# Zeroing two key buffers later on GpSimd, with a new written-out order of all operations, in a two-layer attention and token-MLP kernel

## The chip, the core and the metric

The kernel runs on one core of a Trainium2 chip. The metric is device microseconds of one execution. Four runs of the kernel before gave 458.5, 462.82, 458.71 and 455.29 us, a median of 458.61 us. The core has a matrix engine (TensorE, "PE" in the profile), three engines for elementwise work (VectorE "DVE", ScalarE "ACT", GpSimd "POOL") and a sync engine (SyncE, "SP", whose queue of DMA issues is "SPq").

## The reference

The input `x` has 2048 tokens of 512 numbers, in bf16. Two equal layers follow one another. The first half of a layer is causal attention in a sliding window of 256 tokens, with 32 heads of 16 numbers; the second is an MLP that mixes tokens.

```python
def _A_ref(x, wqkv, wo):                       # attention, H = 32, Dh = 16, W = 256
    qkv = (x @ wqkv).reshape(B, S, 3, H, Dh)   # then q, k, v per head
    scores = einsum("bhqd,bhkd->bhqk", q, k) * Dh ** -0.5
    mask = (i - j >= 0) & (i - j < W)
    p = softmax(where(mask, scores, -1e9))
    return einsum("bhqk,bhkd->bhqd", p, v) ... @ wo

def _B_ref(x, w1, b1, w2, b2):                 # token-mixing MLP, F = 1792
    u = gelu(einsum("bsd,sf->bdf", layernorm(x), w1) + b1)
    return transpose(einsum("bdf,fs->bds", u, w2) + b2)

for _ in range(2):
    x = x + _A_ref(layernorm(x), A_wqkv, A_wo)
    x = x + _B_ref(layernorm(x), B_w1, B_b1, B_w2, B_b2)
```

## The kernel before

**Tiles.** The 2048 tokens lie in `x_sb` as 16 blocks of 128 tokens on the partitions. Four blocks make a group `m`. A block is normalised on VectorE: statistics (`stat`, L479), their aggregate (`agg`, L481), the power -1/2 on GpSimd (`rstd`, L492) and a subtract-and-multiply into `xh_sb` (`xh`, L499). The first group is turned by TensorE (`ftr`, L557) and copied to `xhT` (`evt`, L564 and L566); later groups are turned by DMA (`tr`, L550). Projections give q, k and v (`fq`, `fk` through L521, `fv` L627).

**The key buffers.** Keys go into `kbd`, three slots of 128 x 4096 bf16 in a block-diagonal form: for each head pair, the half that belongs to the other head must be zero. The first group writes its slot in full from PSUM, times a 0/1 column (`evka`, L587 and L589). Later groups put the keys into a staging tile `stg` (`evk`) and then into `kbd` (`kz`), in one of three ways: eight small DMAs that write only the own half (L607), or two multiplications by the 0/1 column on GpSimd or VectorE (both L612). The DMAs need the rest of the slot to be zero, so slots 1 and 2 are zeroed once (`zk`, L461), and every `kz` waits for that. The ones columns in the value buffers `vb` are written once too (`one`, L465 on GpSimd or VectorE, L468 on ScalarE).

**Attention.** A layer has 76 score steps (`sc`, L690). Each fills four PSUM banks, and ScalarE turns them into probabilities with two exponentials (`exp`, L705); GpSimd multiplies the diagonal parts by a mask (`mask`, L723); TensorE multiplies by the values (`pv`, L740). VectorE transposes the sums (`od`, L760), takes reciprocals (`rec`, L764), GpSimd or VectorE multiplies (`prod`, L766), VectorE transposes back (`od2`, L771). The output projection (`fwo`) is added to `x_sb` (`res`, L782).

**MLP.** The first product is made in parts: `fu` steps (two matmuls each, through L521) run between the score steps, and the last four token blocks follow after the attention (`ful`, L861). Gelu is on ScalarE (L876), the second product is `fy` (L521), added to `x_sb` by `resy` (L888). Weights stream through SP's queue (`w1` L796, `w2` L808).

**What sets the order.** The program text makes a list of 2457 operations with their dependencies. `begin_order` (L53) unpacks the strings in `ORDER` into a permutation of that list, and for each operation the choice among its forms (which engine runs it). `Graph.replay` (L184) gives each engine its operations in this order; `Graph.emit` (L205) writes them with the semaphore waits that the dependencies and the reuse of buffers need. So each engine runs a fixed list, strictly in order, and only waits couple the lists. In the lists below, `name.n` is the n-th operation of that kind in the program text.

Of the kernel before, what the change touches and what calls it, by code (L numbers as in the profile page):

```python
# [14 lines left out]
ORDER = (
    'c-',
    'qBQF^KER6&>00{+|aEn85s?4+@Bn3Vl#Og$fr6I3R)oD)c~w3l|C~Ac6`NE>x&cp@0Y~RJd@030t_>!i5V5T)1%IVha}zxNzaZ#THv^;lhQBSL',
    'AxvUVAt1{r{4mkU^G4GrBYPo_o(3^9mu9+c?j0QE-egLAvb+iqdNR)^$I)ZmQsp?M8CrcgQrQEQ%xe$n8i`6u3^?bsW`}Eah&!xNBO?wl!-',
    'uC##h#HSRP`mS+|FxL0=FqEPqS8ztFpErPq1DOC+$9Q%G-OgdH7Dm%I!M`qLxTJ6*{qDWDcX4A24W|M~N8oDS;vb=+z$ho-',
    'M%o?=O@An&M|I~Ie!l?6o%%i|xKdwd5<(>yltYv5J^0~8+Y(AdZHn;eQKRy%>TkyrW=__L;+h&_AA9p#cmdn8)U1n)_ahEQt&3BnyBnddeMk8%',  # L20
    '9(HK)ILfG)8w9B&BEx1%jnbhlZ9(T)59LKAba&K(Ybe$9O_?Tr`xp5__$l;~@D91Y%$LlOjl&V^?GD$Mo3)<Nq(lYS5MgQ1tdr_+_nX0PH^Td`',
    'Yw>+OSnG?^G<+daeav0xZrW_2-',
    'vi$Yh_YJL~>4vUZHfpN<(U5ogf9+94r&Ol|*3oqY0R4>a)CXM@6>*BDQ&~24J53Yel0;b)>35WiT$W|>o*oW^0s6Q<?C=4td%gbd{^6c}M0e}%',
    'eE+ywE|*2IS+|OfOPwTHE;pM5Hk!|8^E+rWLLTPxWHGy2C)3H~?+KaBMr1gdFBa3uY+~Ev(R4Dm-',
    '8k+KZp@qE?Xd4S1JmrAC672C<Ux?7oj?zN?<WadiJxY+tw%xNdDaKd_Xk~{5WUSIGR3h;nU->)YO1E`m9`>K8q#bw*KAFa$hYEPFkI`m(B%QA-',
    'xgi!l_hbbIKF2r2{>m_Xj%FwO;X46T+VE@sj9N0s+=)Xk`A(ANRrAJ)0Skh2Y4PH05NqwpX&hHc&sXtG#JQIq35}-',
    '>+e&}l`x8UK;8qaikzqEy=^<T23Dd04LYjYXxQLqmbsz?R1ztH-S$cv??k4+j)tnM?7hO5OO1<nu$iLi8Xr+6iHvmFd^ex3*o@LyPS9|erPa-',
    '0ahTnw{lTDrgYi4eSe`SWGj$OVf^y#Eh!BjR76@wkVd$GqqHqp#sO>T-',
    'Uc{>FOf`&1Ro)ILx<R^Sm9~}V5&}EgFhnDhnh=o@1hypt|DcW(@fL2nDvBZ!MM>fYLfOFblPWpp?U+2;4#V!pFl>{S*}~jug)PVT2~)u-',
    'bR!<yoTBxbv97EjGR?(tsA_~zPRKXxeI63%!_V;LcJ{ukO2dEzSMsr$&8n1Pt}Dw`UdZAm1(JqIBHwqmXe)(bu)^53yG}K#a2MScW&1ZsM`<Oi',  # L30
    'mK7jh@hu4<&ular-!#CTBjt`{(V><!MpeZWMYi8J8vFaE3>h-',
    '?hxx+;Ja2Ci(uvwVHXS1cia?P>$>3}PFptWzTlVRnHI)&lOK_01eV_Vmh09oOw>fy}aE3%SSu7Uo&6-W$-',
    'QVBK@?z+DcOLNP+bPLKF&&Qvw}Vj-1mn>!_{eqLe*Y#iFhYXa>yAii@uN%+ZcveD*$xRw0V#h>Q@qS@rsJ_T)_^sEAA(RTy-',
    '+C=>|seERaLo;ZJF&>%W9gYV>r5Q>J3F`N|IzXZO}(TJVH1^?!nyee`UKKf^W3hYQ<N&X6VjGN;lPdvV%|>4Y47Q$1>1FUFr+vFWFqzI!IQg)2',
    'SB6fu<RUR-',
    '1deq}iTFpiE@x*GteL_2;wc41D3U={%j!K^0>VhB=#z)6rP$%C;z3xEVI7In;nRv^ki;b~n@M4VS*J#$ZWlpWf`~!^6IJpXWhOU8_KEwKJ_;%d',
    ')eqfHSHS#a0yE-b%S-',
    '^)gBFKDOeH=f%i%ea|y`ABr%KD7C2?hebiXz_;P>p_XM@P0%+Yg5GM%VzI3tY&=~ol&6?Y<!_Fo^cvl+NV$p$DWD2^Jv{-',
    'Tk2Mt|mpMzu0MN#SbA346?-6Ipy`oUMme8LTgrw;N@->V{$9B9A`*)qBDp3S-',
    'v&n%&aiwWts9`_BNoUaVJd7QO5EshMwj3vlBDY~cka48QvZ{`bDiMZ~7@DD~-f@1A4hKs21Wv|BeAqWt(~iyl_8;4g*=(9?+r-',  # L40
    'EqSi8l8(QrH&L-EfC?fDGKswnfKEb_ef%Op+9f*FjVl+uPQN0E=v2Ve2paAt31xg~nuR@~+dSu`-d)Ah+j1vfC3;H26Oc2KU!5`}!3-',
    'KixMsDLP?Fh-uZFOn3fWCVSj=pPXyFoC9%X}ddu&R`HmnTeZTuhpumFy!1sk!^=g5VqTaT{4lI%u3?86K6BnC(xiqJsl*ri!=+Ur>ikTJ|eBfR',
    'FN&Yb1P>`KTQn{8&u>f{BzkAK85pdvtg9Nxh58i1(jTvbME@H8Anqxx!WJ`ZiDe^HJffRKCD(d{)m|CBFD*d_{&sv^F@+d11LE=0rKRiVnJzHZ',
    'O1_<PE&?DbV&^dWTx4)C~Y?S4NZw4659qWXvmmvLAdTwtZW1#eMA9)4;=l6O%R07PJO}1XY63n)3^Av%TpIWPaQX{3(v##ufKk~?AfLI*Uyh1*',
    'sAswTwgu+zq*WJTt~Iq)63Hh-f-',
    '=$?b+@#u+*MH5MZ5WcZ7FOOC2M7_q43=;_KOA;W%CcgXhTcYv6<zXr2s&9|E&p2ZY{4{>DJKf?Bw8M|d@Rgs=Vr#9O3~?xHg=wb})u=NQgO6kc',
    'aWc=6@RB?0}ER{uorjiWy{TC06#Md4+lc7{s0DznS|oD<<RDO{o!F2J5JI4AyXR)kmPKMj@tTdRL*2F~NPXZ&lYM7+vH?W({|q^#9WOnDx-RNl',
    'Kwshz72pWdDj#V5G2@amg4WeU{8Pe0+AhV}Y&O!X7PPLKMj_fijabmZQrP^f<boR^qRQPkeB>lL-m;a-4ycY>{U9RR)x>AHgOg>m?-',
    'E~n>31kN+h7(A_o>#z7FT**xROADa(10sA0=#t6WlMA(@3oq$D)k*CQU28Atz4Go8htDO|HR1ZOsGYf5d!g_JxZ3rC!l&2#^0V@lv|e>yL;(p`',
    't6s*>GJR5w7mX3Fj=N_uxmaAB6NG<DNQ8fDw)SOqg7Bl?{Ex-%lGrQJ75-)83*f>}a_YYt%|8MANJS<'  # L50
)

def begin_order(n):  # L53
# [260 lines left out]
def bass_interleave_layers__sliding_block__mixer_token_mlp__prompt_kernel(  # L314
# [27 lines left out]
    with es:  # L342
# [70 lines left out]
        def load_w(i, a, b):  # L413
# [23 lines left out]
        for h in range(2):  # L437
# [15 lines left out]
        for i, m, c in ((1, 1.0, 0.0), (2, -1.0, 1.0), (3, -1.0, 1.0)):
            op("vector", lambda e, i=i, m=m, c=c: e.tensor_scalar(ldm[:, i, :], ldm[:, 0, :], m, c, op0=ALU.mult, op1=ALU.add),
               reads=["ld0"], writes=[f"ld{i}"])
# [1 line left out]


        ONES = [("one", i) for i in range(3)]
        for i in range(1, 3):  # L460
            op("gpsimd:zk", lambda e, i=i: e.memset(kbd[:, i].bitcast(dt.float32), 0.0), reads=["mhalf"], writes=["zk"], cost=1900,  # L461
               alts=[("vector", lambda e, i=i: e.memset(kbd[:, i].bitcast(dt.float32), 0.0), 2200)])
        two_ones = 1.0 + 0x3F80 / 2.0 ** 23
        for i in range(3):
            f_one = lambda e, i=i: e.memset(vb[:, i].bitcast(dt.float32)[:, :, :, 8:16], two_ones)  # L465
# [499 lines left out]
```

## Time and profile before

| what | us |
|---|---|
| median of four runs | 458.61 (455.29 to 462.82) |
| the profiled execution, its whole time | 459.31 |
| its span from first to last instruction | 457.5 |
| TensorE busy | 417.8 (91%) |
| ScalarE busy | 326.0 (71%) |
| VectorE busy | 302.7 (66%) |
| GpSimd busy | 224.7 (49%) |

The span is all that the profile's pages show; 1.81 us of the execution lie around it. The page has these parts: busy time of each engine; the span in 40 slices of 11.4 us with the busy share of each engine in tenths; the DMA queues; the chain of work that ended last, followed back from the last instruction; the costliest groups of instructions with what ended the idle time before them; and the DMA issues. Windows of the trace can be asked for in the same terms: a timeline in order of time, the waits, one line's instructions, the chain within a window, or the busy time of each engine in given stretches.

Attention of the first layer lies between about 12 and 168 us, its MLP runs to about 207 us, attention of the second layer to about 377 us, and the rest is the second MLP and the output.

### The profile page before, as it was taken

To read this page: it belongs to the slowest core of one execution; us is meant where nothing else is said; L and a number is where in the kernel's file an instruction comes from. 1 tells how busy PE (TensorE), PEld (TensorE's weight loads), DVE (VectorE), ACT (ScalarE), POOL (GpSimd) and SP (SyncE) were. 2 spreads that over 40 slices of the span, in tenths; PEclk is the share of its full clock that TensorE was granted. 3 is DMA by queue.
4 is the path that set the end of the run, shared out by engine and by line. 5 is a ranking of instruction groups with operands and counts; after the bars stand their busy time and mean duration, and the time that the engine had idled before them with its cause. 6 is when DMAs were issued, how large, how long until landed. Compare 5 with 4: busy or idle time off the path is not lost.

```text
span 457.5 us, 14679 instructions
## 1 busy us (share of the span) xinstructions
PE 417.8 (91%) x6346; PEld 201.1 (44%) x6412; DVE 302.7 (66%) x551; ACT 326.0 (71%) x377; POOL 224.7 (49%) x335
## 2 busy tenths in 40 slices
PE   6878878799898999999999999998899989999997
PEld 5644534334343444444545434444344334444443
DVE  6898779777995669754747777677865567531214
ACT  5999979999998960714898989998899961250000
POOL 6556856665867651000557668586776751000000
PEclk9899999999999999999999999999999999999999
DMA  8251434201141368330230323146221447673532
GB/s 252 71 95 24 110 94 58 28 3 27 27 110 30 102 175 234 111 97 24 59 81 15 63 68 56 39 73 102 52 60 48 99 114 209 173 205 105 148 117 92
DMA packets 99744, 41.74 MB, mean 91 GB/s; under 512 B 38240, under 2 KB 99680, under 8 KB 99680
## 3 DMA queue, kind: packets, MB, share of 16 engines
q1 hardware_dynamic: 99680, 40.80, 35.8%
q8 instruction: 51, 0.84, 0.8%
q14 instruction: 13, 0.11, 0.1%
HBM read 33.56 MB, written 2.10 MB: 78 GB/s over the span
## 4 chain that ended last, share of the span: by engine, by line
PE 59%; ACT 14%; DVE 11%; SPq 6%; DMA 4%; issue 2%; POOL 2%
PE PS L521 38%; ACT pt L705 13%; PE PS L861 7%; PE PS L690 6%; PE PS L740 4%; SPq L607 4%; DVE xh_sb L499 3%; PE PS L627 3%; DVE stats L479 2%; DVE x_sb L782 2%; DVE rl L760 2%; SPq L796 1%; DMA w1b<-in_B_w_dram 1%; POOL pt L723 1%; SPq L550 1%
## 5 line engine op out<-in xcount | busy, mean ns | idle before, releaser
L705 ACT ACTIVATE pt<-PS 128x1024 bf16<-128x1024 f32 (+1 forms) x304 | 282.5, 1042 | 22.0 <-PE PS L690 21.1
L723 POOL TENSOR_TENSOR pt<-pt,ldm 128x256 int32<-128x256 int32 (+2 forms) x268 | 176.8, 682 | 96.9 <-ACT pt L705 93.3
L521 PE MATMUL PS<-xh_sb,w1b 128*128 128x512 bf16 x259 | 65.5, 380 | 6.7 <-issue 3.2
L521 PE MATMUL PS<-uT,w2b 128*128 128x512 bf16 x267 | 66.7, 380 | 1.8 <-issue 0.8
L690 PE MATMUL PS<-qT,kbd 32*128 32x256 bf16 (+4 forms) x1488 | 60.4, 252 | 8.0 <-ACT pt L705 4.4
L521 PE MATMUL PS<-xhT,wqkv 128*128 128x512 bf16 (+1 forms) x233 | 54.5, 361 | 8.6 <-DMA xhT<-xh_sb 3.0
L888 DVE SCALAR_TENSOR_TENSOR x_sb<-PS,b2col,x_sb 128x512 bf16<-128x512 f32 x32 | 23.5, 745 | 55.3 <-PE PS L521 53.6
L492 POOL TENSOR_TENSOR rstd<-agg,mhalf 128x2 f32<-128x2 f32 (+1 forms) x33 | 23.7, 719 | 62.2 <-DVE agg L481 62.2
L760 DVE STREAM_TRANSPOSE rl<-PS 128x1024 f32<-128x1024 f32 x32 | 39.8, 1245 | 16.3 <-PE PS L740 16.0
L690 PEld LDWEIGHTS PS<-qT,kbd 32*128 32x128 bf16 x1488 | 22.1, 92 | 62.3 <-ACT pt L705 43.2
L876 ACT ACTIVATE uT<-rl,b1col 128x512 bf16<-128x512 f32 x28 | 18.4, 712 | 39.7 <-DVE rl L872 39.7
L740 PE MATMUL PS<-pt,vb 64*32 64x320 bf16 (+4 forms) x2976 | 44.8, 253 | 1.8 <-POOL pt L723 0.8
L479 DVE BATCH_NORM_STATS2 stats<-x_sb 128x6 f32<-128x512 bf16 x64 | 42.8, 680 | 1.6 <-DMA x_sb<-in_A_x_dram 1.0
L521 PE MATMUL PS<-uT,pt 128*128 128x512 bf16 x159 | 40.2, 379 | 0.3
L521 PEld LDWEIGHTS PS<-uT,w2b 128*128 128x128 bf16 x276 | 25.3, 98 | 32.5 <-issue 2.9
L521 PEld LDWEIGHTS PS<-xh_sb,w1b 128*128 128x128 bf16 x278 | 23.4, 97 | 35.9 <-issue 8.7
L740 PEld LDWEIGHTS PS<-pt,vb 64*32 64x32 bf16 x2976 | 29.6, 90 | 19.7 <-POOL pt L723 9.7
L861 PE MATMUL PS<-xh_sb,w1b 128*128 128x512 bf16 x164 | 37.4, 379 | 0.4
L627 PE MATMUL PS<-wqkv,xhT 128*64 128x256 bf16 x512 | 34.7, 276 | 2.8 <-DVE stats L479 1.2
L499 DVE TENSOR_SCALAR xh_sb<-x_sb,agg,rstd 128x512 bf16<-128x512 bf16 x64 | 31.1, 514 | 8.2 <-POOL rstd L492 8.1
L521 PEld LDWEIGHTS PS<-xhT,wqkv 128*128 128x128 bf16 x254 | 21.6, 100 | 29.8 <-issue 5.4
L627 PEld LDWEIGHTS PS<-wqkv,xhT 128*64 128x64 bf16 x512 | 25.5, 109 | 11.0 <-issue 3.6
(69 smaller groups left out, 345.6 us busy)
## 6 DMA issues: line engine op xcount, KB each, us to landing
w1b<-in_B_w_dram SPq DMA_DIRECT2D x112, 128.0 KB, 2.9
w2b<-in_B_w_dram SPq DMA_DIRECT2D x70, 128.0 KB, 2.5
pt<-in_B_w_dram SPq DMA_DIRECT2D x42, 128.0 KB, 3.2
out_dram<-x_sb SPq DMA_DIRECT2D x16, 128.0 KB, 1.9
kbd<-stg SPq DMA_DIRECT2D x120, 16.0 KB, 1.9
x_sb<-in_A_x_dram SPq DMA_DIRECT2D x3, 512.0 KB, 8.0
wqkv<-in_A_wqkv_dram SPq DMA_DIRECT2D x4, 256.0 KB, 4.2
wqkv<-in_A_wqkv_dram SPq DMA_DIRECT2D x1, 512.0 KB, 7.2
```

The lines of the kernel that those rows point to most:

```text
L479: op("vector:stat", lambda e: e.bn_stats(st[:, 0:6], x_sb[:, t, :]), reads=[f"x{t}"], writes=[("st", i)], cost=dve_cost(512), after=late_s ...
L492: op("gpsimd:rstd", lambda e: e.tensor_tensor(rstd[:, t0:t1, 0], agg[:, t0:t1, 1], mhalf[:, 0:1].to_broadcast([P, t1 - t0]), op=ALU.pow), ...
L499: op("vector:xh", lambda e: e.tensor_scalar(xh_sb[:, t, :], x_sb[:, t, :], agg[:, t, 0:1], rstd[:, t, :], op0=ALU.subtract, op1=ALU.mult), ...
L521: return e.matmul(o, lhsT=w, rhs=x, start=start, stop=stop, skip_group_check=True)
L627: last = e.matmul(bank(ft)[64 * j:64 * j + 64, sc * 256:(sc + 1) * 256], lhsT=xhT[:, tx.slot, c, tok:tok + 64], rhs=wqkv[:, c, 1024:1536]. ...
L690: last = e.matmul(bank(tt[r // 2], r % 2)[:, base + c0 * 64:base + (c0 + n) * 64], lhsT=kbd[32 * r:32 * r + 32, tk.slot, o, jj].rearrange( ...
L705: op("scalar:exp", lambda e, ts=ts, tp=tp, i=i, cols=cols: e.activation(probs(tp)[:, i, 0:cols, :], pair(ts)[:, :, 0:cols].rearrange("p r ...
L723: return e.tensor_tensor(v, v, m, op=ALU.mult)
L740: last = e.matmul(bank(t, h)[32 * r:32 * r + 32, i + q0 * 64:i + (q0 + n) * 64], lhsT=vb[64 * h:64 * h + 64, tk.slot, jj, 4 * o + r, :], r ...
L760: op("vector:od", lambda e, t=tod, tr=tr: e.transpose(rl[:, tr.slot:tr.slot + 2].rearrange("p a b -> p (a b)"), pair(t)), reads=[(tod, i) ...
L861: last = e.matmul(bank(tu, tt), lhsT=v()[:, sc - b0, k0 + tt * P:k0 + (tt + 1) * P], rhs=xh_sb[:, sc, :], start=(sc == b0), stop=(sc == NT ...
L888: op("vector:resy", lambda e: e.scalar_tensor_tensor(x_sb[:, t, :], bank(ft), b2col[:, t:t + 1], x_sb[:, t, :], op0=ALU.add, op1=ALU.add), ...
```

## The change

The two `zk` operations are no longer written ahead of the first normalisation. They stand in the program text after the first group's projections, and they read `xh3`, the fourth normalised token block, in place of `mhalf`: so they may not begin before the first four blocks are normalised. No operation is added or taken out. The strings in `ORDER` are new throughout.

```diff
 ORDER = (
-    'c-',
-    'qBQF^KER6&>00{+|aEn85s?4+@Bn3Vl#Og$fr6I3R)oD)c~w3l|C~Ac6`NE>x&cp@0Y~RJd@030t_>!i5V5T)1%IVha}zxNzaZ#THv^;lhQBSL',
...
+    'c-qZYFNixy7Oo^UyS-',
+    '2cbx;enP#n!s3w=<cMT<V@U0U=(M2m<PEn4(JL_|a%MC6W$9JGjN5fRZMA_oyUh=_=Yh=_=Yh=|BR#E20i=3qp`h=>vQGLy+<elxSTEDLupOs4',
...
         ONES = [("one", i) for i in range(3)]
-        for i in range(1, 3):
-            op("gpsimd:zk", lambda e, i=i: e.memset(kbd[:, i].bitcast(dt.float32), 0.0), reads=["mhalf"], writes=["zk"], cost=1900,
-               alts=[("vector", lambda e, i=i: e.memset(kbd[:, i].bitcast(dt.float32), 0.0), 2200)])
...
             prepare(0)
+            if not layer:
+                for i in range(1, 3):
+                    op("gpsimd:zk", lambda e, i=i: e.memset(kbd[:, i].bitcast(dt.float32), 0.0), reads=["xh3"], writes=["zk"], cost=1900,
+                       alts=[("vector", lambda e, i=i: e.memset(kbd[:, i].bitcast(dt.float32), 0.0), 2200)])
             for c, (qs, nq) in enumerate(CHUNKS[layer]):
```

Unpacked by the rule of `begin_order`, the two strings give these beginnings of the engines' lists:

```
GpSimd before: ident x3, mhalf, tri, zk.0, rstd.0, rstd.1, tri, one.1, zk.1, rstd.2, one.2, mask.1, mask.3, mask.0, mask.2, mask.5, rstd.4, mask.4, rstd.3, mask.7
GpSimd after:  ident x3, tri x2, mhalf, one.2, rstd.1, rstd.0, rstd.2, mask.1, zk.0, mask.3, mask.4, mask.0, rstd.3, mask.6, rstd.4, mask.2, mask.5, mask.7, mask.8, zk.1, mask.9
VectorE before: eps x2, half0, stat.0, agg.0, stat.1, agg.1, par0, par1, xh.0, xh.1, evt.1, half1, evka.0, evka.1, ld0, stat.2, stat.3
VectorE after:  half1, eps x2, par0, half0, stat.1, agg.1, stat.0, agg.0, ld0 x2, xh.1, xh.0, par1, evt.0, ld3, ld2, evka.1, evka.0, evq.0
ScalarE before: one.0, tab.0, evt.0, evka.2, evka.3, evq.0, evka.7, evka.6, exp.0
ScalarE after:  tab.0, one.0, one.1, evt.1, evka.3, evka.2, evka.4, evka.5, exp.0
SP before: ... kz.0, kz.3, w1 x3, tr.6, w1 x2, tr.7, tr.4, tr.5, w1, kz.2, w1 x6, b2, b1, kz.6, tr.11, tr.10, w1 x2, tr.8, tr.9, kz.9, kz.8, w1 ...
SP after:  ... kz.0, wo, b2, kz.2, w1 x2, tr.4, tr.7, tr.6, w1, tr.5, w1 x3, kz.3, w1 x7, kz.4, tr.9, tr.11, tr.8, tr.10, kz.5, kz.6, w1, kz.7, kz.8, w1 ...
```

Over the whole kernel the score steps keep their order among themselves, and 50 operations run on another engine. Where the counts differ:

| operations | layer 1 before | layer 1 after | layer 2 before | layer 2 after |
|---|---|---|---|---|
| `kz` on SP / VectorE / GpSimd | 7 / 4 / 1 | 11 / 1 / 0 | 8 / 3 / 1 | 6 / 2 / 4 |
| `prod` on VectorE / GpSimd | 9 / 7 | 5 / 11 | 7 / 9 | 10 / 6 |
| `one` on GpSimd / ScalarE | 2 / 1 | 1 / 2 | | |
| `fu` steps after the 76th score step of the layer | 21 | 23 | 9 | 7 |

More of the change, by code (lines that the diff above doesn't have):

```diff
@@ L15 @@
 ORDER = (
-    'c-',
-    'qBQF^KER6&>00{+|aEn85s?4+@Bn3Vl#Og$fr6I3R)oD)c~w3l|C~Ac6`NE>x&cp@0Y~RJd@030t_>!i5V5T)1%IVha}zxNzaZ#THv^;lhQBSL',
[L18 to L50, printed above, removed]
+    'c-qZYFNixy7Oo^UyS-',
@@ new lines @@
+    '2cbx;enP#n!s3w=<cMT<V@U0U=(M2m<PEn4(JL_|a%MC6W$9JGjN5fRZMA_oyUh=_=Yh=_=Yh=|BR#E20i=3qp`h=>vQGLy+<elxSTEDLupOs4',
+    '<5u72-(-}hAzLO};>I7u8w!z4-',
+    'K*n&V_rR)bk{)jY;Orez2zn4bY2+E!;m*rzEuI~47>^OIaPz2XOBivqJ2Z8N`p6%FMN0(Ap$~Dz;VJ}xpY#j`dHl=L08>{ttE&HOM+e)<YFp8q',
+    'SYW2Dy&!k?BJKXUcUI`kqUg54wb<0(bV^6uRi>XqSP}6bJ{%SSld_I48IJEj!)40F8{e#>+TqipoMK?E`3$&g4>-',
+    'APji%i&(^W}Om^E`b%J51P=xvo9Pv8gQDZD;0gw@Y`OG+he;g=C9Hb2*!f#_z^d(BWV_<Ww@HdOelrITMVJ=!WQgw`{kYHXE~MH)|yIv|ewwDx',
+    'CAwbz!OXy4&q85bDr}UbCqZs>g$y!GKU2_4`pZuEzCNtyU#}X*R-e$b+C-',
@@ new lines @@
+    'mANEo8tPHG9Lpa_HDH8uUyvyD{Bp(feZOqo+})9gxXzYXewj#5xl5N)qSF>_*beuyj8M`xEbIE(d3cP&C<y3A@PG?l=ejs7oQK8UG=<;>Hzenj',
+    '@qCcy8qqW@Hw<kwI#5cx`~BhZ(7)gB)3kE{WXRp!8a}ts*3A*#dp04P-F9tRa<|=X*M!5J>+8FR-JaYo@0QEmOj|6r8>e1hubkPe=FI0a;6ct<',
+    'bs4XgE;G&YW}77KZZFTfX4|qFqS^a%v(e~eje0vx5={%WdKGYqSNbxlR;y7p995_`HcfwE_RHl?$K1Pi%XQ4_oit6RdC0&^DU}cui{WrwUyq?{',
+    '#zuLyI_MLIImd~w-Dq0Nwwn#&64PuELOdJ7kzp7`j%`;YrGnU;07h8TbW7hZHX9)GW__?G6Ky($0(f6ACb-}o#-',
+    'vOb`xfyi<+U)BTn2tcS4<fjl(_cRvTbFWdwR_0ObBLC%hW(==#c>GLemPAGOQ`fgkh=GO2P!^5FF~AOmvM<jnQ52euujIO^gPQFf5FxX$t|b=3',
@@ new lines @@
+    '_P+j1VfILEi0k2|*~7+cbsckq`(m#L@9cAPpIev5bxM2<6k(m=Y9Nj2Jo@$Q*LAZk9z!q!ErQ^)MQb#(rd0%4IB(Y`d;(G^~UOBy?`uz$Jm)8k',
+    '4$Y#teGmR@GyUiIE~icN|C8L2G&t=mwSoE-',
+    '=TDm;mj>Mqq9jfP*+brcu)%_((pY{bmT!>7ZJz*3`g<rVDhHTn*6CjF6_uZxG_9WhP1DdM;zUK@>4~1GHX!d?Yd3K-',
+    'BrFR$Bn`7Let}9*LVjH1Y<4xt762zIRAsL$77<JXCQVsKIfaa=Gkzp5xFk3>8HPi#^9sB@@)7=vJ8uC_bJ3ivm}KG~_IssT3k_Ddl-',
+    '>Hk|_edEnWedr$w)0aMx*&2_W+S9pME2Xv63AuIO*@`Yj0Z=g>7cC}jF-rmh^yLNpIGKZOyg;w|$5AfB*s@F$DYcLoGL4Z&#98NrM*mLrM+aFM',
+    'xb;si|AcE3%tJOMWhg)c1d%&$$id}a$$BmS+xHcHX7V6?G3(6!6{U{84T&YFSW9VayJvS%>74M1rf3yXdHVlCg_Yoo6bsWpOwE!A$M&WI5s0)&',
@@ new lines @@
+    'Hx6Wp_+l0||`0&7xx-',
+    '*qh|5WN9cHgld#(VdEG@_<%s#eQXu&PqsE{*oqeHw<AMGsq3Jya@6At||SuGV_5*PH7*aPfJ%TrL|t>HfZ6U#(Z1Lyarj_Wi}e-',
+    'U(rCH>6kT=YxK)pZ9tr6eIb_yT*6-s9UL2(lk5nHuF}i)9Ezyokllp;`T_!XAL6^J4PIYid6hyzE5SfTC2GmO<G77X{Ta=mXQKRCkfE3iWt-',
+    '#xvr}_uIKHy_t9ox7)mX+DX?H_7~dhJlo%NhXaJ%5S*E&wbK0;wfMs>8np>}1pgr&-i0R{WI{g#IXh_Izdz8DTfmY$-',
+    '6i*uyG#m|q&ck6c==WJaXE4vS3D#(8Nxh?KX*-',
+    'UlA?y!fy(XoMqaGXrYGJ$W`o8PCo^(>GwLlmYcAhw<wN6~Afa*D`gq8gs|N9<2f*cQyvttMyYY0QAeKCj6asi!9XSSM5l%ZlMx07YVEb+@MX*S',
@@ new lines @@
+    'unZE)ds8&$y$-',
+    '3C}xz1C<pn1+BndTinc5VBQPfD1sfm?<+x{5#lAz+>orPU&xH*4}~EkYTi1g(Ge_j)G{|?IKM_0&y`0f1>aKxY~%4*sX0wBZSc+p3P>hsMn36M',
+    'kmj)hMHa{O4G=%`}NTGIf|m#^Qq@@t?ZOheYw23v1-<A);E!*`e<TcRL*>j2V&-',
+    'xb;%Db+8^h^JhrW{+cjGqRt!^21mP5KCX<Pj2oHo9X$J^k{k^!m6L_)$R?LU%;WW##e8PIu>t?gpYykuqm@)>!wVKU(EyMG<pAIlMSGkgQqIy(',
+    '|ny8i~o##MEqJiGbgI-S)neV3#g5Ms}^ia$q#=!_LLU4wDy(oNfdW_Gr@n?@eJ%msHpN|W#D?a~wIxUq-$FHZui*-ux-',
+    '&Oh=zP|qYd|te)<6R+N6^q3W3jXTyq=<^8VhLScJ)K=$zO;CJ{J6rY+NV==$}66VKebSJIw)M=fln2|^};#hr*M32`4hZLrBdlV(l6*1(981A^',
@@ L51 @@
+    'D31JpP~3BUYk0jRXmk_uA=aU4Hs`OoF|HY)p*w_DiuGj{^S0NpL6?_dgpn(X|wRs<rf@%hV^NhZ&{2!nAS@!Dtw};FQ9zI^Zz$W?{!)HoL$A@N',
+    'j^tX6^loG717m~DKCj9v7JyUKB?;&j<fj`&mg_B^mTBBR~Nu%FL?ec;diiJva9qgtdso|KCqsPY_N*rnP8=J6Q@qzF|c?N7`n(j{e8&M0>V$6!',
+    '(S5QWTkHjQ#fuZ_+tZv8%Ga#xm3c>qQX!#{<8f~#{8kIil?07NArHZik}mUFO9#9`2v?qlLbf%?*vkKBZ*Ssa>CCyUg%Odqx*%f3UB3p31{IaH',
+    'oKp<EnW=bY}V&Dy%_S_JI~(n;tLlBbKw@Rbbe~Q_-6C{CH7GI@4NfY`U&uMxA~=u{>r~g{#RxElK2ml#!ET'
 )
```

## The prediction

> **What bounds the kernel.** I read the page's busy table, then the busy time by stretches, then the chain, and last the timelines of the first 25 us.
>
> ```profile
> PE 417.8 (91%) x6346; PEld 201.1 (44%) x6412; DVE 302.7 (66%) x551; ACT 326.0 (71%) x377; POOL 224.7 (49%) x335
> ACT  5999979999998960714898989998899961250000
> ```
>
> TensorE is busy in 417.8 of 457.5 us, so all orders together can win 39.7 us at most. But the second line says that ScalarE is nearly full from the second slice to the thirteenth (the first layer's attention). The stretches show the same:
>
> ```profile
> 0.00:12.80 12.80, 8.33 (x74) 6.73 (x75) 8.51 (x20) 7.10 (x10) 6.93 (x15) 0.91 0.84 262
> 12.80:40.00 27.20, 22.17 (x557) 14.66 (x557) 22.96 (x53) 26.02 (x38) 16.82 (x24) 0.98 0.29 57
> ...
> 80.00:100.00 20.00, 16.45 (x347) 6.98 (x343) 14.89 (x24) 19.93 (x22) 13.24 (x20) 1.00 0.13 20
> ...
> 240.00:260.00 20.00, 19.68 (x357) 10.22 (x352) 15.95 (x29) 18.36 (x22) 14.16 (x22) 1.00 0.13 25
> ...
> 300.00:320.00 20.00, 17.48 (x373) 8.71 (x372) 15.41 (x28) 18.30 (x22) 14.31 (x22) 1.00 0.60 94
> ```
>
> The columns are the stretch and its length, then the busy time of PE, PEld, DVE, ACT and POOL. Between 12.8 and 40 us ScalarE is idle 1.2 us of 27.2; between 80 and 100, 0.07 of 20, while TensorE is idle 3.5. So the first layer's attention is a train of exponentials: if it departs earlier, it arrives earlier. In the second layer TensorE is the fuller engine.
>
> The chain shows what holds the departure:
>
> ```profile
> 4.73 0.57 POOL rstd L492
> 5.31 0.03 issue
> 5.33 3.02 DVE xh_sb L499
> 8.35 0.04 issue
> 8.40 0.41 PE PS L557 x4
> ...
> 12.81 0.91 ACT pt L705
> ```
>
> One normalisation stands there with 3.02 us. Over its 64 runs that line has a median of 407 ns (310 the least), so 3.02 - 0.41 = 2.6 us are waiting. GpSimd's timeline at that moment:
>
> ```profile
> 5.26 0.30 POOL L446 TENSOR_SCALAR_AFFINE_SELECT tri<-tri 128x128 bf16<-128x128 bf16 x1
> 5.50 0.95 POOL L465 MEMSET vb<- 128x1024 f32 x1
> 6.39 1.81 POOL L461 MEMSET kbd<- 128x2048 f32 x1
> ```
>
> They run with no gap until 8.20, and the normalisation ends 0.15 after that. It waits not for one GpSimd instruction but for the whole row.
>
> **A rule beside this row.** The Trainium skill, "SBUF — State Buffer", section "Who interferes with whom", says that a GpSimd operation and a VectorE operation in a two-port mode (tensor_scalar among them) exclude one another, for the whole instruction, by who starts first. Read by instruction, the waiting normalisation would have got in when the select ended at 5.56, and deferring the zeroing would win nothing; the trace has it behind two more memsets. The measurement decides, and by the rule alone the first term below would be 0.
>
> **Part 1, the head.** In the new lists the zeroing is gone from there, and one `vb` memset (0.95 us) stands ahead of the first `rstd`. Behind the two rstd comes `rstd.2`, which waits for statistics of blocks 2 and 3, so GpSimd is idle while the two blocks are normalised. The chain again by its own rows: aggregates at 4.67, rstd to 5.3, two normalisations at 0.4 to about 6.1, transposition 0.41 and copy 0.44 to 7.0, where 9.32 stood before: 2.3 us. ScalarE takes a second `vb` fill (1.91 us, L468): its table load 1.28 and two fills end at about 6.0, before its copy is due, so this costs nothing; with that cover gone it costs up to 1.9. Next late would be the weights: of the 256 KB loads, median 4.2 us to landing, the third is issued by 3.24, so 7.44, which would leave 1.9. The other end is 2.6, the whole wait. If `xh` meets both rstd (0.56 each) instead, it gains 1.5. **Taken: -2.3, bounds -2.6 to -1.5.** It arrives at the end of the train because ScalarE waited only 8.2 us for scores from 12.8 to 170.
>
> **Part 2, the zeroing in its new place.** Twice 1.81 = 3.62 us among the first masks; a `vb` memset of 0.95 leaves that stretch.
>
> ```profile
> 13.72 0.95 POOL L465 MEMSET vb<- 128x1024 f32 x1
> 17.73 3.36 POOL L723 TENSOR_TENSOR pt<-pt,ldm 128x128 int32<-128x128 int32 x5 [3.06 <-DVE ldm L454]
> 21.05 0.70 POOL L492 TENSOR_TENSOR rstd<-agg,mhalf 128x2 f32<-128x2 f32 x1
> 21.72 0.45 POOL L723 TENSOR_TENSOR pt<-pt,ldm 128x128 int32<-128x128 int32 x1
> ```
>
> GpSimd was idle for 3.06 us before the masks (the bracket), and `zk.0` stands just there: its `xh3` comes right behind the mask constant that ended that idle time. So the first zeroing is hidden. `zk.1` stands between `mask.8` and `mask.9`, where idle pieces of 0.84 and 0.22 and later 1.10 and 1.81 follow. Behind `zk.0` are queued mask.3, mask.4, mask.0 and `rstd.3` (awaited by blocks 4 and 5), behind `zk.1` the masks of the next `pv`. The key copies that wait for the zeros begin at 34.49 on SP: 10 us of room. Bounds: 0 and 3.62 - 0.95 = +2.7; no gain is possible, as GpSimd only gets work here. **Taken: +0.3**, near the hidden end, since the 4.1 us of idle time is more than the 2.7 added.
>
> **Part 3, work moved past the last score step.** Two more `fu` steps stand behind the 76th score step of layer 1 (23 for 21). Four such matmuls take 0.86, a step of two 0.43: **+0.86**, because past that point TensorE alone sets the time. In layer 2 the same two move the other way, but there TensorE is the fuller engine already: 0.
>
> **Part 4, SP's queue.** In layer 1 four more `kz` go by SP.
>
> ```profile
> 34.49 11.26 SPq L607 DMA_DIRECT2D kbd<-stg x16
> 45.79 2.97 SPq L796 DMA_DIRECT2D w1b<-in_B_w_dram x3
> 48.81 1.23 SPq L550 DMA_TRANSPOSE xhT<-xh_sb x1
> ```
>
> Each is eight issues at a median of 0.60, 4.8 us; four are 19.2 us. Cover is there: SP issues nothing from 82.3 to 101.7, 113.2 to 123.2 and 130.1 to 132.1. VectorE loses three of them and four net `prod`, which it does not miss at 66%; GpSimd waited 93 us in all for exponentials and has room for the four `prod` (1.06 each). Taken 0. Without cover one `kz` is late by its own 4.8. In layer 2 SP has two fewer; the scores waited for such copies 1.0 us in all. Bounds -1.0 to +4.8.
>
> The transposes of blocks 8 to 11 stood on the chain here (DMA 4.46 us at 55.19, TensorE waiting 2.7). In the new list `tr.4, tr.7, tr.6` stand behind two `w1` loads and not three, but also behind `wo` (0.58) and `b2` (half of 3.31 = 1.65). Three transposes now follow one another, and `xh.15`, the last of that group before, comes first in VectorE's new list. Bounds -2.7 (wait gone) to +2.2 (the two loads in full). **Taken: -0.7**, a quarter of the wait.
>
> **Part 5, the rest of the order.** All lists are new, which no row prices. An estimate of the spread: TensorE's idle time in the eight 20-us stretches from 220 to 380 is 0.5, 0.3, 1.5, 0.8, 2.5, 1.6, 0.9 and 1.9, a standard deviation of 0.75. If each of 16 such stretches is drawn anew, the sum moves by 0.75 x sqrt(2 x 16) = 4.2 us, either way. Taken 0.
>
> **Sum:** -2.3 + 0.3 + 0.86 - 0.7 = -1.8 on the profiled execution's 459.3, which gives 457.5. That execution lies 0.7 above the median of the four runs, so by the median 458.6 - 1.8 = **456.8 us**. What a measurement of this kernel can tell from no change is about 1%, 4.6 us; this forecast lies within it.
>
> **Rivals.**
> - *Faster by over 1%* (0.24). The order packs better everywhere: the head in full (-2.6), the transposes' wait gone (-2.7), 2.0 off the 7.6 us that TensorE idles in the four worst stretches of layer 2 (260 to 280, 300 to 340, 360 to 380), and +0.86: -6.4, about 452.2. For it: fewer VectorE multiplications that can wait for GpSimd (`kz` L612 takes from 248 to 1198 ns there). Against it: the PE rows after 168 us are full already.
> - *Slower by over 1%* (0.22). SP falls behind in layer 1: `kz.4`, four transposes, `kz.5`, `kz.6`, `kz.7`, `kz.8` follow in one row. Five score steps use one `kz`, some 10 us of exponentials, so SP at 4.8 keeps up once it has begun; it decides when the row begins over 5 us after its keys are due. Then one `kz` (+4.8) and the two loads (+2.2) are on the path; with the head's -2.3 and +0.86 this is +5.6, about 464.2. For it: four times 4.8 us more in that queue. Against it: the idle stretches above.
> - *The change doesn't do what it says* (0.13, within 1%): the normalisation meets another row of GpSimd instructions, the memset and both rstd among them, and the head gains nothing: +0.3 + 0.86 = +1.2, about 459.8.
> - The forecast itself has 0.41.
>
> **Range and chances.** The forecast's own spread is 1.28 x 4.2 = 5.4 either way, 451.4 to 462.2. Slower reaches 464.2 and faster 452.2 with their own spread, so the range that leaves 2 in 10 out is 450.8 to 464.3. Faster by over 1%: 0.24; within 1%: 0.41 + 0.13 = 0.54; slower by over 1%: 0.22.
>
> **What would show it.** Part 1: no normalisation above 0.6 us before 9 us, the first projections at about 7.0 and the first exponential at about 10.4 (12.7 before). Part 2: zeroing rows at about 14 and 22 us with masks close behind and no `pv` waiting over 0.6 for them. Part 3: the gap from the 76th exponential pair to gelu wider by 0.9. Part 4: a score step waiting for a key DMA over 1 us would be the slower rival. The prediction is wrong if the train departs 2.3 earlier and doesn't arrive earlier, with ScalarE idle over 11 us between departure and 168, or if the second layer's PE idle time moves by over 5 us.

## The result and the profile after

The changed kernel takes 457.29 us (median of 48 runs) where the kernel before takes 458.82 (72 runs): a ratio of 0.9955, 95% interval 0.9937 to 0.9973, 2.1 us less. Forecast was 1.8 us less. The ratio compares the executions within 1.5% of each kernel's fastest; by the medians of all of them the difference is 1.5 us. The profiled execution of the changed kernel took 453.47 us, 3.8 less than its median; so its stages are read beside other traces of the same lists below.

The busy table and ScalarE's slices of the page after:

```profile
span 451.7 us, 14744 instructions
PE 416.7 (92%) x6375; PEld 200.5 (44%) x6440; DVE 302.3 (67%) x545; ACT 324.6 (72%) x374; POOL 226.7 (50%) x339
ACT  7989979999998960624999999999999980520000
```

The busy times are as before, within 2 us. At the head, the chain (start, length, what) no longer holds a normalisation:

```profile
1.77 4.02 PE PS L397 x36
5.79 0.44 PE PS L553 x4
6.23 0.02 issue
6.25 0.59 ACT xhT L562
6.85 0.36 issue
7.21 1.93 PE PS L517 x16
9.14 0.02 issue
9.16 0.84 ACT kbd L585 x2
10.00 2.32 ACT pt L701 x3
```

The warming matmuls lead over to the first transposition at 5.79, the projections start at 7.21 (9.32 before), and the first exponential at 9.89 (12.70 before). But further on the chain of the same trace has this:

```profile
20.30 0.33 DVE qT L575
20.64 2.89 DVE xh_sb L495 x2
23.53 1.16 DVE rl L756
24.69 0.14 issue
24.82 0.43 PE PS L686 x12
25.25 0.02 issue
25.27 3.77 ACT pt L701 x4
```

And GpSimd's timeline at that moment:

```profile
18.74 2.90 POOL L719 TENSOR_TENSOR pt<-pt,ldm 128x256 int32<-128x256 int32 x4
21.58 1.80 POOL L904 MEMSET kbd<- 128x2048 f32 x1
```

Two normalisations take 2.89 us, up to 0.15 after the end of the moved zeroing (23.38); the second began at 20.97, while a mask ran to 21.63, and the zeroing followed that mask without a gap. The transposition of sums behind them (`rl`) is late, a score step waits 2.10 us for it, and ScalarE stands idle for 1.97. The stall of the head was moved to 21 us.

**Stages.** From each trace: start of the first exponential, the stretch of layer 1's 152 exponentials, the gap to layer 2's first, its 152, and the rest.

| trace | first exp | layer 1 | gap | layer 2 | to the end | span |
|---|---|---|---|---|---|---|
| before | 12.70 | 153.87 | 46.16 | 161.87 | 82.9 | 457.5 |
| after | 9.89 | 154.26 | 49.04 | 156.28 | 82.3 | 451.7 |
| after, profiled again | 9.56 | 155.98 | 49.04 | 156.26 | 82.3 | 453.1 |

### The profile page after: what moved, and what is told of

It is laid out like the page before. It is cut to its first block, busy times and chain, and to the rows that moved or that the text cites. A ratio compares the mean times of both kernels' runs of the same rounds, so it can differ in the third digit from the quotient of the medians.

```text
span 451.7 us, 14744 instructions
## 1 busy us (share of the span) xinstructions
PE 416.7 (92%) x6375; PEld 200.5 (44%) x6440; DVE 302.3 (67%) x545; ACT 324.6 (72%) x374; POOL 226.7 (50%) x339
## 4 chain that ended last, share of the span: by engine, by line
PE 65%; ACT 19%; DVE 7%; SPq 3%; POOL 2%; issue 2%; DMA 2%; POOLq 0%
PE PS L517 38%; ACT pt L701 18%; PE PS L857 7%; PE PS L686 6%; PE PS L736 5%; PE PS L623 5%; SPq L603 2%; DVE xh_sb L495 2%; POOL pt L719 2%; DVE rl L756 2%; PE PS L519 2%; SPq L792 1%; DMA xhT<-xh_sb 1%; PE PS L397 1%; DVE x_sb L778 1%
## 5 line engine op out<-in xcount | busy, mean ns | idle before, releaser
L719 POOL TENSOR_TENSOR pt<-pt,ldm 128x256 int32<-128x256 int32 (+1 forms) x268 | 176.3, 680 | 85.3 <-ACT pt L701 83.5
L517 PE MATMUL PS<-xh_sb,w1b 128*128 128x512 bf16 x250 | 63.0, 380 | 4.8 <-issue 2.5
L517 PE MATMUL PS<-uT,w2b 128*128 128x512 bf16 x266 | 65.5, 379 | 1.2 <-issue 0.8
L488 POOL TENSOR_TENSOR rstd<-agg,mhalf 128x2 f32<-128x2 f32 (+1 forms) x33 | 22.6, 690 | 67.0 <-DVE agg L477 66.8
L517 PE MATMUL PS<-xhT,wqkv 128*128 128x512 bf16 (+1 forms) x210 | 49.2, 356 | 5.3 <-issue 2.4
L857 PE MATMUL PS<-xh_sb,w1b 128*128 128x512 bf16 x165 | 37.9, 379 | 0.2
L517 PEld LDWEIGHTS PS<-xh_sb,w1b 128*128 128x128 bf16 x268 | 22.4, 98 | 33.1 <-issue 8.7
L517 PEld LDWEIGHTS PS<-xhT,wqkv 128*128 128x128 bf16 x232 | 19.2, 98 | 24.0 <-issue 4.2
```

Of the source, the lines that this page charges most:

```text
L488: op("gpsimd:rstd", lambda e: e.tensor_tensor(rstd[:, t0:t1, 0], agg[:, t0:t1, 1], mhalf[:, 0:1].to_broadcast([P, t1 - t0]), op=ALU.pow), ...
L517: return e.matmul(o, lhsT=w, rhs=x, start=start, stop=stop, skip_group_check=True)
L719: return e.tensor_tensor(v, v, m, op=ALU.mult)
L857: last = e.matmul(bank(tu, tt), lhsT=v()[:, sc - b0, k0 + tt * P:k0 + (tt + 1) * P], rhs=xh_sb[:, sc, :], start=(sc == b0), stop=(sc == NT ...
```

## The experiments

All edits act on the list that `begin_order` returns, with two helpers ahead of `g.replay(order)`: `waits_for(o, d)` adds `d` to the dependencies of `o`; `behind(o, d)` moves `o` straight behind `d`. Ratios are to the kernel before, from five rounds, with 95% intervals.

**1. The old lists with two waits at the head.**

```diff
+for o in (kind("one", 1), kind("zk", 1)):
+    waits_for(o, kind("xh", 1))
```

> The old lists, unchanged, with two waits added: the vb memset one.1 and the zeroing zk.1 wait on GpSimd for the second normalisation xh.1. Theory (the head sets the departure of the train): GpSimd pauses after the affine select that ends at 5.55, xh.1 ends by 6.0 instead of 8.34, the first exponential starts at about 10.4 instead of 12.70, and the whole time falls by 1.5 to 2.3 us (ratio 0.995 to 0.997). Rival (the new order of the other operations is what pays, the head's gain is lost behind it): the head shortens just the same, but the whole time stays within 0.5 us of the kernel before.

Measured: **0.9954 (0.9928 to 0.998)**, first exponential at 9.36. By the ratios, two waits in the old lists bring as much as the whole change. VectorE's and GpSimd's timelines:

```profile
4.75 0.96 DVE L499 TENSOR_SCALAR xh_sb<-x_sb,agg,rstd 128x512 bf16<-128x512 bf16 x2
```

```profile
5.22 0.29 POOL L446 TENSOR_SCALAR_AFFINE_SELECT tri<-tri 128x128 bf16<-128x128 bf16 x1
5.77 0.95 POOL L465 MEMSET vb<- 128x1024 f32 x1 [0.25 <-DVE xh_sb L499]
6.65 1.81 POOL L461 MEMSET kbd<- 128x2048 f32 x1
```

Both normalisations are done by 5.71, at 0.41 us each; the affine select beside the second costs it nothing here. Of the 3.3 us at the start 2.1 arrive at the end by the ratio, 0.9 to 3.3 by its interval. In this trace 4.28 us of idle time of ScalarE stand before 59 us (in the kernel before 2.89, ahead of 61.6). TensorE's line where it resumes there, first before, then here:

```profile
59.92 1.24 PE L521 MATMUL PS<-xhT,wqkv 128*128 128x512 bf16 x5 [2.72 <-DMA xhT<-xh_sb]
```

```profile
55.88 2.67 PE L521 MATMUL PS<-xhT,wqkv 128*128 128x512 bf16 x6 [2.48 <-DMA xhT<-xh_sb]
```

TensorE waits no longer for the transposes than before (2.48 for 2.72 us), and they land 3.8 us earlier. What is longer is the projections behind them, at a granted clock of 0.50 from 55.99 to 59.41.

**2. Only zk.1 waits.**

```diff
+waits_for(kind("zk", 1), kind("xh", 1))
```

> The old lists with one wait added: only zk.1 waits for xh.1; the vb memset stays straight behind the affine select. If each memset holds VectorE's normalisation for its own time, and a row without a gap adds up, xh.1 ends 0.4 after the vb memset's end at 6.45, so at about 6.9, and the first exponential starts at about 11.2. If only the zeroing of kbd blocks, xh.1 ends at about 5.8. If the wait at the head has nothing to do with zk.1 following closely, xh.1 still ends near 8.3. The whole time: a gain of 1.0 to 1.5 us by the head theory, nothing by the rival.

Measured: **0.9959 (0.9921 to 0.9996)**, first exponential at 10.23.

```profile
4.77 1.80 DVE L499 TENSOR_SCALAR xh_sb<-x_sb,agg,rstd 128x512 bf16<-128x512 bf16 x2
```

```profile
5.48 0.95 POOL L465 MEMSET vb<- 128x1024 f32 x1
6.64 1.80 POOL L461 MEMSET kbd<- 128x2048 f32 x1 [0.20 <-DVE xh_sb L499]
```

The pair now ends at 6.57, 0.14 after the `vb` memset, where it ended 0.15 after the second memset before. So each memset holds the normalisation, and a memset without a wait ahead of it follows the first with no gap. One wait on GpSimd is enough to let VectorE through. ScalarE's wait before 59 us is 0.46 in this trace; it idles 1.28 and 1.35 us at 20 and 33 us instead.

**3. The new order with the zeroing back at the head.**

```diff
+for i in range(2):
+    kind("zk", i).deps = [d for d in kind("zk", i).deps if d.kind != "xh"]
+    behind(kind("zk", i), kind("rstd", 0) if i else kind("one", 2))
```

> The new order with the two zeroings put back at the head: zk.0 ahead of the two rstd, zk.1 right behind them, neither waiting for a normalisation; everything else as in the changed kernel. Head theory: a normalisation again stands 1.8 us or more behind zk.1, the first exponential starts at 11.7 to 12.5 instead of 9.9, and the whole time is 1 to 2.5 us above the changed kernel, so level with the kernel before (ratio to before 0.998 to 1.002). Rival (the order pays): it keeps most of the gain, ratio 0.994 to 0.996.

Measured: **0.9977 (0.9947 to 1.0007)**, first exponential at 12.70 again. The pair of normalisations ends 0.14 after `zk.1` (VectorE's and GpSimd's timelines):

```profile
5.59 2.39 DVE L495 TENSOR_SCALAR xh_sb<-x_sb,agg,rstd 128x512 bf16<-128x512 bf16 x2 [0.19 <-POOL rstd L488]
```

```profile
6.03 1.81 POOL L904 MEMSET kbd<- 128x2048 f32 x1
```

By the ratios half of the gain, 1.0 us, goes with 2.8 us at the head, a difference that lies within the intervals; the other half stays, but its interval takes in 1. The traces show what stands against the 2.8: without a zeroing at 21 us there is no stall there, and layer 1 takes 152.31 us instead of 154.26. In these two traces the move won 2.8 and paid 1.95 back.

**4. The moved zk.1 waits as well.**

```diff
+behind(kind("zk", 1), kind("xh", 4))
+waits_for(kind("zk", 1), kind("xh", 4))
```

> The changed kernel with zk.1 waiting for xh.4 and standing directly behind mask.2, ahead of mask.5, mask.7 and mask.8. In the changed kernel xh.4 stands 2.55 us behind zk.1 at 20.97, the transposition of the sums behind it is late, and a score step waits 2.1 us. Theory: xh.4 takes 0.4 to 0.5, the score step's wait of 2.1 and ScalarE's idle 1.97 at 25 us are gone, and the whole time falls by 1 to 2 us below the changed kernel (ratio to before 0.991 to 0.994). Rival (the next wait takes its place, the later masks hold the next product with the values): the wait moves to mask.9 or mask.10 and the time stays within 0.5 us of the changed kernel.

Measured: **0.9917 (0.9883 to 0.995)**, 1.7 us better than the change by the two ratios, whose intervals overlap. The normalisations take 0.40 to 0.41 each, GpSimd idles 1.84 for them, and ScalarE's idle time at 25 us is gone:

```profile
20.29 0.72 DVE L495 TENSOR_SCALAR xh_sb<-x_sb,agg,rstd 128x512 bf16<-128x512 bf16 x2
20.93 1.24 DVE L756 STREAM_TRANSPOSE rl<-PS 128x1024 f32<-128x1024 f32 x1
```

But in this trace ScalarE then stands still before 59.29, when the changed kernel resumed at 59.12 too:

```profile
59.29 1.94 ACT L701 ACTIVATE pt<-PS 128x1024 bf16<-128x1024 f32 x2 [4.54 <-PE PS L686]
```

The train was 1.9 us earlier at its 41st exponential, but the transposes landed at 56.73, hardly earlier than in the changed kernel (56.89), and the eight matmuls behind them took 1.92 us for 1.05, at a granted clock of 0.50 from 55.64.

**5. The second gate.** In the changed kernel's SP queue (timeline: start, length, issues) the key copies `kz.2` stand ahead of the transposes, whose last input was normalised at 45.0:

```profile
39.85 8.10 SPq L603 DMA_DIRECT2D kbd<-stg x8
47.99 1.66 SPq L792 DMA_DIRECT2D w1b<-in_B_w_dram x2
49.69 3.85 SPq L546 DMA_TRANSPOSE xhT<-xh_sb x3
53.59 0.59 SPq L792 DMA_DIRECT2D w1b<-in_B_w_dram x1
54.23 1.90 SPq L546 DMA_TRANSPOSE xhT<-xh_sb x1
```

```diff
+late = [kind("w1", 4), kind("w1", 7), kind("kz", 2), kind("w1", 12)]
+for d in reversed(late):
+    behind(d, kind("tr", 5))
```

> The changed kernel, with one edit in SP's list alone: the four transposes of blocks 8 to 11 stand ahead of w1.4, w1.7, kz.2 and w1.12, not behind them. In the changed kernel these blocks are normalised by 45.0 us, but their transposes are issued from 49.7 to 56.1, behind the eight issues of kz.2, and ScalarE stands idle for 2.37 us up to 59.1. Theory (a second gate in SP's queue takes back a part of the head's gain): the transposes are issued from about 45 on, the idle time before 59 is gone, the time falls by 1 to 2.4 us (ratio to before 0.990 to 0.994). Rival (the projections and value evictions behind the transposes are the gate, or kz.2 is then late for the score steps that need it): the idle time stays over 1.5 us there or appears behind 60, and the time stays within 0.5 us of the changed kernel.

Measured: **0.9881 (0.9832 to 0.9931)**, the most of a single edit, and clear of the change's own interval. SP's and ScalarE's timelines:

```profile
41.82 6.32 SPq L546 DMA_TRANSPOSE xhT<-xh_sb x4
48.19 2.05 SPq L792 DMA_DIRECT2D w1b<-in_B_w_dram x2
50.28 5.84 SPq L603 DMA_DIRECT2D kbd<-stg x8
```

```profile
57.34 5.61 ACT L701 ACTIVATE pt<-PS 128x1024 bf16<-128x1024 f32 x6 [0.46 <-PE PS L686]
```

The idle time fell from 2.37 to 0.46 us, and layer 1 from 154.26 to 151.34; neither trace has a halved clock within layer 1.

**6. Both edits together.** The edits of 4 and 5.

> The two edits on the changed kernel together: zk.1 waits for xh.4 ahead of mask.5, and the four transposes stand ahead of kz.2 in SP's list. With zk.1 alone out of the way ScalarE's idle time before 59 us was 4.54 instead of 2.37: the gain of 2 us up to there was given back. Theory of the second gate: now both are open, ScalarE idles less than 1.5 us before 60, and the time is 2 to 4 us below the changed kernel (ratio to before 0.984 to 0.991). Rival: as with zk.1 alone, ratio 0.990 to 0.993.

Measured: **0.987 (0.983 to 0.9911)**, 452.23 us: not to be told from edit 5 alone. ScalarE idled 1.28 and 1.51 us at 15 and 29 us in its trace. The stall at 59 us is gone, but this doesn't show that the two gains add up. Edits 5 and 6 are the fastest versions found, 5 to 6 us below the kernel before.

**7. Both gates in the old lists.** Edit 1, and the transposes ahead of kz.3 and five weight loads.

```diff
+for o in (kind("one", 1), kind("zk", 1)):
+    waits_for(o, kind("xh", 1))
+for d in (kind("w1", 6), kind("w1", 12), kind("w1", 0), kind("w1", 13), kind("w1", 4), kind("kz", 3)):
+    behind(d, kind("tr", 5))
```

> The old lists with the two waits at the head (one.1 and zk.1 wait for xh.1) and with the transposes of blocks 8 to 11 ahead of kz.3 and the weight loads in SP's list. With the waits alone the first exponential was 3.3 us earlier, but 4.28 us of idle time stood before 59 us. Theory of the second gate: that idle time falls below 2, and the time falls by 2 to 3.5 us more than with the waits alone (ratio to before 0.988 to 0.992). Rival (the new order is needed for it): no further gain, ratio 0.994 to 0.997.

Measured: **1.0048 (1.0021 to 1.0075)**, slower; both expectations missed. `kz.2` now came behind kz.3 and the loads, and SP's queue had stood idle from 36.77 to 44.47 ahead of the transposes (why, see 10). TensorE's waits between 55 and 72 us:

```profile
PE PS L690 <- DMA kbd<-stg: 5.6, 1, 5.6
```

**8. Four key copies back on their engines.**

```diff
+for i, alt in ((4, 2), (5, 2), (7, 2), (11, 1)):
+    k = [e[0] for e in order].index(kind("kz", i).idx)
+    order[k] = (order[k][0], alt)
```

> The changed kernel with four key copies of layer 1 back on the engines that they had before: kz.4, kz.5 and kz.7 on VectorE, kz.11 on GpSimd, 32 DMA issues fewer on SP. The prediction took their move to SP as free. If so the time stays within 0.7 us of the changed kernel (ratio to before 0.994 to 0.997). Rival (SP's queue is behind because of them): 1 to 2 us faster. Third: VectorE's copies, which can wait for GpSimd, hold the sums and the time is 1 to 2 us slower.

Measured: **0.995 (0.992 to 0.998)**, as the changed kernel, within 1.4 us either way. No price of their move to SP shows, as predicted.

**9. Early transposes, zeroing at the head.** The edits of 5 and 3.

> The changed kernel with the four transposes early in SP's list and with both zeroings back at the head, as in the run that put them there. With the transposes late the zeroing at the head cost about 1 us of the 2.8 by which the first exponential was later. Theory (the second gate hid the rest): with the gate open the head counts nearly in full, 1.8 to 2.8 us above the run with early transposes alone (ratio to before 0.992 to 0.995). Rival (something else takes it back): within 1 us of that run, ratio 0.987 to 0.990.

Measured: **0.9921 (0.9888 to 0.9953)**, 1.8 us above edit 5 (the two intervals overlap). The first exponential is 2.85 later and layer 1 is 1.4 shorter, again without a stall at 21 us.

**10. Early transposes in the old lists alone.**

```diff
+for d in (kind("w1", 6), kind("w1", 12), kind("w1", 0), kind("w1", 13), kind("w1", 4), kind("kz", 3), kind("kz", 2)):
+    behind(d, kind("tr", 5))
```

> The old lists without any wait at the head; in SP's list alone the four transposes of blocks 8 to 11 come first, then kz.2, kz.3, and then the weight loads. Before, ScalarE stood idle for 2.89 us up to 61.6. Theory: that idle time goes, 1.5 to 2.9 us faster (ratio 0.994 to 0.997). Rival (the copies or the weight loads that are now later are waited for, as kz.2 was): level or slower, ratio 0.999 to 1.006.

Measured: **1.0134 (1.0089 to 1.0179)**. TensorE's timeline:

```profile
80.62 0.38 PE L521 MATMUL PS<-xh_sb,w1b 128*128 128x512 bf16 x1 [0.65 <-ACT pt L705]
86.75 2.74 PE L521 MATMUL PS<-xh_sb,w1b 128*128 128x512 bf16 x6 [5.75 <-DMA w1b<-in_B_w_dram]
```

The load that it waits for was not put back: it stands further on in SP's queue (`w1.2`, behind `kz.6` and two transposes) and was issued at 84.40, where the kernel before issued it at 77.84. SP's timeline shows where the queue lost this time:

```profile
34.78 5.49 SPq L607 DMA_DIRECT2D kbd<-stg x8
47.93 6.04 SPq L550 DMA_TRANSPOSE xhT<-xh_sb x4
```

It stands idle from 40.27 to 47.93, because the old lists normalise blocks 8 to 11 only from 46.7 to 49.3, and what is queued behind the transposes comes late. The new lists normalise them between 35.7 and 45.1, and in experiment 5 the queue was idle only from 40.12 to 41.82.

**11. The same with the waits at the head.** The edits of 1 and 10.

> The old lists with the waits at the head and the four transposes early, and with kz.2 straight behind them, ahead of kz.3 and the weight loads: in the last try of this kind a score step waited 5.6 us for kz.2. Theory: that wait goes, both gates are open in the old lists, and the time is 3.5 to 5.5 us below the kernel before (ratio 0.988 to 0.992), as good as the new order with the same edits. Rival (the rest of the new order is worth something of its own): ratio 0.993 to 0.997.

Measured: **1.0058 (1.003 to 1.0085)**; the same wait for weights, 5.0 us, and the same idle queue, from 38.07 to 45.85. Early transposes won 0.7% in the new lists and lost 1.3% in the old. The edits are not quite equal (three loads and one key copy put back there, five and two here), but the traces show the difference in the inputs: a queue that issues in order gains by an early transpose only where its input is ready when the queue arrives.

**12. The changed kernel profiled again.**

> The changed kernel without any edit, profiled once more, because its profiled execution (453.47) lies 3.8 us below its median. In all traces so far the stretches behind the first layer's exponentials agree within 0.3 us for the same lists: 49.0 from the last exponential of layer 1 to the first of layer 2, 156.3 from there to the last one, 82.3 to the end. Theory: only the stretch of the first layer's 152 exponentials (154.3 in the first profile) scatters between executions, so a slower execution shows 155 to 158 there and the same numbers in the rest. Rival: the second layer's 156.3 was a lucky one too and comes out 158 or more.

Measured: 454.85 us; its stages are in the table above. As expected, layer 1 differs, and nothing behind it. All eight traces with new lists agree on the gap (49.0 to 49.1), layer 2 (156.1 to 156.3) and the end (82.2 to 82.3); the six with old lists on 46.0 to 46.2, 160.3 to 162.2 and 82.4 to 83.8 us.

## Why the prediction was right, and where not

The sum was right, -1.8 for -2.1, and its first reason is shown. Three of its terms were not right; they cancelled, so that the sum came so close is in part luck.

- **Part 1, -2.3:** the departure gained 2.8, with the mechanism as told (experiments 1 to 3). By the ratios it did not pass through in full: 2.1 of 3.3 in the old lists, 1.0 of 2.8 in the new, 1.8 of 2.85 with the transposes out of the way, each with an interval of over 1 us either way. "It arrives at the end of the train because ScalarE waited only 8.2 us" was the weak step: the sum of the waits before says little about the waits of an earlier train. Before 59 us ScalarE idled 4.28 and 4.54 us in 1 and 4; in 4 the transposes in SP's queue landed no earlier for it, in both the clock was halved there. In 2 the same wait was 0.46.
- **Part 2, +0.3:** this step failed. The working looked for masks that would be late, found 10 us of room, and did not apply its own finding of Part 1 to the new place: a memset without a wait holds VectorE's normalisation wherever it stands. The first zeroing was hidden as worked (12.48 to 14.28, GpSimd idle for 0.43 behind it). For the second the trace has 1.97 us of idle ScalarE; a wait for xh.4 takes it away, worth 1.7 by ratios whose intervals overlap. What was late next was not a mask but a transposition of sums.
- **Part 3, +0.86:** the gap grew by 2.88, for besides two `fu` steps it also took two more `fy`, two `fk` and one `fq` step: seven of 0.43 are 3.0. Most of these are work that layer 2 then no longer has.
- **Part 4:** no price of the four copies shows (8). The rival "SP falls behind" did not come true, but its price is real: 5.6 and 5.75 us when copies or loads were issued too late (7, 10). The transposes were put at -0.7; ScalarE's wait there fell by 0.5, from 2.89 to 2.37 us, and 5 shows that the rest could go too.
- **Part 5, 0 +- 4.2:** mis-sized. Behind layer 1 the traces have +2.88, -5.59 and -0.6, together -3.3: layer 2 is 4 to 6 us shorter with all new lists. The timed runs show less of it: with the zeroing at the head, the new order is worth 1.1 us, between 2.4 and -0.3. One reason is the clock of the timed runs (below). Which part of the order shortens layer 2 was not tried.

Of the prediction's two signs of being wrong, the first came near: in the first profile the train arrived 2.4 us earlier (164.15 for 166.57) with 9.9 us of waiting, in the second 1.0 us earlier with 11.3, over the 11 that were set. TensorE's idle time from layer 2's first exponential to its last fell by 3.2 us, from 10.1 to 6.9, under the 5 that were set.

## What to carry to other kernels

When a stalling operation is moved, ask the question that condemned the old place of the new one: who runs on the engine beside it there? A wait on the blocking engine can be worth more than another place: two waits in the old lists brought as much as 2457 reordered operations. And a gain at the start of a train is kept only as far as the next gate, so look for that gate, here four transposes behind eight small DMA issues, before counting it. Before something is moved forward in a queue that issues in order, look up when its input is ready: until then all that stands behind it waits too.

## What the runs showed of the hardware

**Memsets and masks on GpSimd hold a normalisation, a power does not.** The normalisation in bf16 takes 0.40 to 0.41 us alone and beside a power (before, 4.79 to 5.20, with the power from 4.73 to 5.30). One that begins behind a memset or a mask ends 0.14 to 0.15 us after it. A mask in the kernel before (VectorE's and GpSimd's timelines):

```profile
252.76 0.80 DVE L499 TENSOR_SCALAR xh_sb<-x_sb,agg,rstd 128x512 bf16<-128x512 bf16 x1 [3.15 <-POOL rstd L492]
```

```profile
252.68 0.73 POOL L723 TENSOR_TENSOR pt<-pt,ldm 128x256 int32<-128x256 int32 x1
```

The mask ends at 253.41, the normalisation at 253.56. The 64 normalisations of the fourteen traces that began 0.1 us or more ahead of a mask took at most 0.41. The wait of experiment 5's queue up to 41.82 is of this kind: the normalisation that it needs took from 39.78 to 41.80, beside a mask of 1.8 us.

What sets a memset apart shows where two instructions follow without a gap. A normalisation that had waited for at least 0.25 us came in between two masks in all 89 cases. Between a mask and the zeroing it did not (the changed kernel's two profiles, 5 and 8), nor between the two memsets at the head (before, and 10). Why is not shown. Nor is it shown whether the affine select holds a normalisation: in 1 the second one ended at 5.71, and a hold up to 0.15 after the select (5.51) would not be seen in that. The Trainium skill, "SBUF — State Buffer", section "Who interferes with whom", gives the pair of ports that GpSimd shares with VectorE's two-port modes for a whole instruction to whoever issues first, and excepts no GpSimd operation; the masks agree, a power that lets the normalisation pass and a memset that goes ahead of one that waits do not.

**TensorE's clock halves in steps of 3.41 us after a half-idle step.** Stretches of the traces, cut at these steps (length; busy PE, PEld, DVE, ACT, POOL; granted clock third from the end). Before, at the head:

```profile
6.96:10.37 3.41, 1.45 (x14) 1.18 (x15) 1.93 (x3) 0.41 (x2) 1.24 (x1) 1.00 1.07 347
10.37:13.78 3.41, 3.41 (x27) 2.06 (x26) 2.89 (x9) 2.61 (x7) 0.70 (x2) 0.50 1.04 331
```

The changed kernel in its second profile, at the stall behind the moved zeroing:

```profile
21.59:25.00 3.41, 1.32 (x30) 0.94 (x25) 3.41 (x4) 1.46 (x3) 2.59 (x3) 1.00 0.46 93
25.00:28.42 3.42, 3.12 (x96) 1.86 (x94) 2.02 (x5) 3.42 (x4) 1.47 (x2) 0.50 0.04 7
```

And in its first, where the step fell otherwise on the wait before 59 us:

```profile
55.05:58.46 3.41, 1.65 (x32) 0.75 (x16) 1.25 (x1) 1.70 (x2) 1.63 (x3) 1.00 0.61 123
```

From where the record of the clock begins (4 to 8 us) up to the last 7 us, all 11 steps of the fourteen traces at full clock with under 1.5 us of busy TensorE were followed by a halved one; of those with 1.5 to 2.0 us some were, and of those with more none. So a wait costs more where it empties a step, and the same wait in the same kernel is followed by a halved step in one execution and not in another. The first profile of the changed kernel had none before its last matmuls, the second had two; the kernel before had one, experiment 10 five. That fits the scatter within layer 1. The Trainium skill, "TensorE: Matmul & The Clock Gate", section "What's actually happening", has a free-running window of 3413 ns and half the clock after an idle one; the length agrees, but here windows with 1.3 to 1.95 us of busy TensorE were enough.

The timed runs have no trace, but each has its granted clock. Of the changed kernel's 39 that the ratio compares, the two at 0.999 and 1.0 took 453.47 and 453.15 us, the eleven at 0.992 a median of 456.01 and the eight at 0.985 458.18: most of the 3.8 us between the first profile and the median go with the clock. Ten of the 39 are at 0.985 or less; of 74 such runs of the kernel before, timed beside the experiments, one is. At 0.995 and more the changed kernel has a median of 453.5 us (7 runs) and the kernel before 457.5 (26). So the new lists save some 4 us where the clock stays nearly full, and about half of that goes again with halved steps. Which waits bring these on in the timed runs is not shown.
